# Expert layers of a Sinkhorn mixture: activations and operand differences held in the PSUM banks in the first pass

## The chip, the cores and the metric

The kernel runs on one core of one Trainium2 chip, in one launch. Times are device microseconds of that core; the times of a kernel are a median over runs, and one execution of it was profiled.

## The reference

```python
def _moe_ref(x, w_gate, w1, w2):                 # x: 3072 x 512, 8 experts, F = 1024
    logits = x @ w_gate
    logits = logits - logits.max()
    P = np.exp(logits)
    for _ in range(8):
        P /= P.sum(1, keepdims=True) + 1e-09
        P /= P.sum(0, keepdims=True) + 1e-09
        P *= N / E
    for e in range(E):
        h = np.maximum(x @ w1[e], 0.0)
        out += P[:, e:e + 1] * (h @ w2[e])

def reference(**kwargs):
    attn_out = _attn_ref(q, k, v, n_global, n_local)    # banded attention, 4 x 8 x 768 x 64
    x = attn_out.transpose(0, 2, 1, 3).reshape(B * S, H * D)
    return _moe_ref(x, w_gate, w1, w2)
```

Banded attention makes the 3072 rows of 512 numbers that go through eight experts. Each expert's two layers are matrix products with a ReLU between them, and a row's result is weighted by its share P of the expert.

## The kernel before

The hidden dimension of all experts is cut into 31 groups of two 128-wide tiles (`groups`, `NG` = 31) and the rows into three passes (`NB` = 3). The first four groups (`PLAIN` = 4) of the first pass run in a stage of their own, between the attention and the loop that the change is about. That loop (`for n, (what, p, x, y) in enumerate(todo)`) runs pass 0 over groups 4 to 29 in 13 pairs, here called chunks, and over group 30, called plain; then passes 1 and 2 over all groups.

Both expert layers are computed by a seven-product (Strassen and Winograd) scheme. Every operand of a product is held as a high part, rounded to a 32-bit matmul format, and a rest (full value minus high part), and every product takes three matmuls per tile. Layer 1 of a group (`layer1_scaled`, "a first" below) makes the products m3, m2, m1, m6, m5, m4 and m7, six matmuls each, in four PSUM banks c, d, a, b (c, d and a are used twice). VectorE puts them together in two running sums t3 and t1; `scaled` applies the ReLU and the share and writes the four blocks h22, h12, h21, h11 to SBUF; the differences d7 = h12 - h22, d5 = h22 - h21, d6 = h12 - d5 and d4 = d6 - h11 are formed from them. Each of the seven results becomes an operand p1 to p7 of layer 2: `high` is a ScalarE cast, `rest` subtracts that cast from the result. In pass 0 (`prepares`) all differences and rests run on VectorE; in passes 1 and 2 on GpSimd.

Layer 2 (`second_layer`) runs over a chunk's two groups in two parts: p3, p7, p5, p1 in the chunk itself, and p6, p4, p2 behind the even first of the next chunk ("behind" below). So the order on TensorE is, chunk by chunk: even first (42 matmuls), behind of the chunk before (36), odd first (42), second (48). Four sums (p3, p7, p6, p4; `SEEDED`) are copied into their bank by ScalarE ahead of the matmuls and copied out behind them; the other three are added by VectorE (L1500).

In pass 0 the weights' operands are made on the way (`make_blocks`): a DMA on SyncE's queue brings a raw tile (`raw`, two buffers), GpSimd forms the scheme's sums (`ext`, and `raw` in place; L1380, L1398), ScalarE casts the high parts (L1410), GpSimd subtracts for the low parts (L1411), and the block `wb` (a ring of five) is also written to DRAM (L1043), from where passes 1 and 2 load it. Blocks are asked for two items of `todo` ahead.

A scheduler orders each engine's instructions, but for those recorded through `Ordered`, which keep the program's order. Line 68 is `Ordered`'s, so that all its operations stand at L68.

Of the kernel before, what the change touches and what calls it, by code (L numbers as in the profile page):

```python
# [17 lines left out]
P = 128  # L18
# [5 lines left out]
UT = 3  # L24
# [572 lines left out]
class Moe:  # L597
# [173 lines left out]
    def layer1_scaled(self, x, blocks, share, full, ops, tmp, ps, tag, waits, used, begins, soon, plain, prepares):  # L771
# [7 lines left out]
        if prepares:  # L779
            gp = Ordered(self.tc, nc.vector).tensor_tensor  # L780
# [97 lines left out]
        rest("p2", h11, other)  # L878

# [116 lines left out]
def pipeline(tc, attention, ident, moe, acc, scratch):  # L996
# [12 lines left out]
    with ExitStack() as top:  # L1009
# [243 lines left out]
        def second(g, hs, halves=(0, 1)):  # L1253
            e, b = groups[g][0], passes[0]
            first_scaled = e != 0 and groups[g - 1][0] == 0
            for i in halves:
                for t in range(WT):
# [3 lines left out]
                    if t == 2:  # L1261
                        beat()
# [8 lines left out]
                    if g == PLAIN - 1:  # L1271
                        u, n = divmod(tt, UT)
                        nc.sync.dma_start(out=y_spill[u][:, n], in_=a)
# [20 lines left out]
        for g in range(PLAIN):  # L1294
# [22 lines left out]
            if g == PLAIN - 1:  # L1317
                spill_rows()
            if g == 1:
                second(*prev, (0,))  # L1320
                second(g, hs, (0,))
                moe.act = nc.scalar
            elif g == 2:
                second(*prev, (1,))
            elif prev is not None:
                second(*prev)
            prev = (g, hs)
        second(*prev)
        load_share(0, groups[PLAIN][0])
# [35 lines left out]

        def make_blocks(g, layer, part):

            e, f = groups[g]
            gp = nc.gpsimd.tensor_tensor
            base, (lo, hi) = 7 * layer, ((0, SPLIT), (SPLIT, 7))[part]  # L1370
            if layer == 0:
                if part == 0:
                    raw = wstage.tile([P, KT, FG * P], F32, name="raw")
                    nc.sync.dma_start(out=raw, in_=moe.w1[e, :, f * P:(f + FG) * P].rearrange("(c p) f -> p c f", p=P))
# [12 lines left out]
            elif g == NG - 1:  # L1387
                raw = wstage.tile([P, FG, DM], F32, name="raw")
                nc.sync.dma_start(out=raw, in_=moe.w2[e, f * P:(f + FG) * P, :].rearrange("(f p) d -> p f d", p=P))
                parts = ((slice(0, 4), raw.rearrange("p f (d c) -> p (f d) c", d=2), None),)  # L1390
            elif part == 0:
                raw = wstage.tile([P, FG, DM], F32, name="raw")
                nc.sync.dma_start(out=raw, in_=moe.w2[e, f * P:(f + FG) * P, :].rearrange("(f p) d -> p f d", p=P))
# [8 lines left out]
            else:  # L1402
                raw = wstage.tile([P, FG, DM], F32, name="raw")
                nc.sync.dma_start(out=raw[:, 0], in_=moe.w2[e, f * P:(f + 1) * P, :])
                nc.sync.dma_start(out=raw[:, 1, 0:FULL], in_=s2_spill[g])
# [14 lines left out]
        def first_layer(p, g):  # L1420
# [15 lines left out]

            return moe.layer1_scaled(ops, lambda i: blocks_of[g, 0, i], share, free if begins else full, ops_of[g], tmp, mps, "h",
# [212 lines left out]
```

## Time and profile before

| | us |
|---|---|
| median of 3 runs (lowest, highest) | 2208.03 (2207.44, 2209.78) |
| the profiled execution: its own time | 2207.4 |
| its span | 2205.5 |
| mean granted TensorE clock, share of full speed | 0.976 |

| engine | busy us | share of the span |
|---|---|---|
| TensorE matmul (PE) | 2091.2 | 95% |
| GpSimd (POOL) | 1660.7 | 75% |
| VectorE (DVE) | 1535.0 | 70% |
| ScalarE (ACT) | 863.2 | 39% |

The page's 40 slices show TensorE at eight or nine tenths up to about 1000 us and at nine or more behind that; VectorE's digits fall there from eight to five or six. The loop begins at 363 us (first matmul of group 4), and pass 0 ends at 1008 us. The rows below are from that stretch, and from pass 1 for comparison. In the timeline rows, the columns are start, duration, engine, line, operation, tiles and count, and in brackets the idle time ahead of it with what ended it.

### The profile page before, as it was taken

To read this page: it belongs to the slowest core of one execution; us is meant where nothing else is said; L and a number is where in the kernel's file an instruction comes from. 1 tells how busy PE (TensorE), PEld (TensorE's weight loads), DVE (VectorE), ACT (ScalarE), POOL (GpSimd) and SP (SyncE) were. 2 spreads that over 40 slices of the span, in tenths; PEclk is the share of its full clock that TensorE was granted. 3 is DMA by queue.
4 is the path that set the end of the run, shared out by engine and by line. 5 is a ranking of instruction groups with operands and counts; after the bars stand their busy time and mean duration, and the time that the engine had idled before them with its cause. 6 is when DMAs were issued, how large, how long until landed. Compare 5 with 4: busy or idle time off the path is not lost.

```text
span 2205.5 us, 30538 instructions
## 1 busy us (share of the span) xinstructions
PE 2091.2 (95%) x10365; PEld 1726.9 (78%) x10365; DVE 1535.0 (70%) x2534; ACT 863.2 (39%) x1832; POOL 1660.7 (75%) x1441
## 2 busy tenths in 40 slices
PE   8999997889888888879999999999999999999998
PEld 6888885667776677768888888888888888888887
DVE  8777775888888888876556655665656655655566
ACT  7777533555554555522322222222142222222221
POOL 6787974887888887884777767676867676767776
PEclk9999998999999899989999999999999999999999
DMA  6777475667666666679656566565785665656564
GB/s 156 211 216 206 156 272 189 222 217 251 225 234 230 229 222 239 219 275 341 210 193 207 179 209 209 201 209 191 281 300 188 210 210 186 212 193 212 182 209 158
DMA packets 229157, 477.49 MB, mean 216 GB/s; under 512 B 107072, under 2 KB 152576, under 8 KB 205696
## 3 DMA queue, kind: packets, MB, share of 16 engines
q1 hardware_dynamic: 228704, 474.40, 63.6%
q8 instruction: 84, 1.38, 0.3%
q0 software_dynamic: 288, 1.05, 0.1%
q14 instruction: 81, 0.66, 0.1%
HBM read 328.75 MB, written 146.64 MB: 216 GB/s over the span
## 4 chain that ended last, share of the span: by engine, by line
PE 68%; POOL 13%; issue 6%; DMA 5%; DVE 4%; ACT 4%; SPq 0%; POOLq 0%; DVEq 0%; ACTq 0%
PE c_acc L124 28%; PE bank_c L124 8%; PE bank_a L124 8%; PE bank_d L124 8%; POOL wb L1411 6%; PE bank_b L124 4%; DMA raw<-in_moe_w_dram 4%; POOL ext L1398 2%; PE o_t L124 2%; POOL ext L1380 2%; ACT p_sb L369 2%; POOL raw L1380 1%; PE o_ps L124 1%; PE s_ps L124 1%; PE y_ps L124 1%
## 5 line engine op out<-in xcount | busy, mean ns | idle before, releaser
L124 PE MATMUL c_acc<-p,wb 128*128 128x512 f32 x2838 | 703.4, 401 | 69.7 <-DVE p L68 65.2
L124 PEld LDWEIGHTS c_acc<-p,wb 128*128 128x128 f32 x2838 | 549.6, 194 | 195.7 <-issue 61.5
L796 ACT CAST p<-full 128x512 fp32r<-128x512 f32 x384 | 226.3, 621 | 697.1 <-DVE full L793 423.9
L1500 DVE TENSOR_TENSOR early<-early,c_acc 128x512 f32<-128x512 f32 x363 | 246.0, 685 | 182.5 <-PE c_acc L124 182.4
L68 POOL TENSOR_TENSOR p<-full,p 128x512 fp32r<-128x512 f32 x270 | 347.8, 1304 | 5.0 <-ACT p L796 4.7
L124 PE MATMUL bank_c<-x,wb 128*128 128x512 f32 x1068 | 275.2, 393 | 16.9 <-ACT wb L1410 10.0
L68 POOL TENSOR_TENSOR early<-full,full 128x512 f32<-128x512 f32 x56 | 72.9, 1301 | 287.6 <-DVE full L793 287.6
L124 PE MATMUL bank_a<-m,wb 128*128 128x512 f32 x1068 | 273.1, 391 | 5.3 <-DVE early L806 4.7
L124 PE MATMUL bank_d<-x,wb 128*128 128x512 f32 x1068 | 273.0, 391 | 0.0
L124 PEld LDWEIGHTS bank_c<-x,wb 128*128 128x128 f32 x1068 | 202.5, 190 | 60.5 <-ACT wb L1410 10.4
L124 PEld LDWEIGHTS bank_a<-m,wb 128*128 128x128 f32 x1068 | 201.3, 189 | 48.5 <-DVE early L806 5.6
L124 PEld LDWEIGHTS bank_d<-x,wb 128*128 128x128 f32 x1068 | 202.0, 189 | 42.4
L68 POOL TENSOR_TENSOR full<-full,full 128x512 f32<-128x512 f32 x172 | 222.8, 1296 | 0.0
L124 PE MATMUL c_acc<-x,wb 128*128 128x512 f32 x774 | 197.6, 390 | 1.6 <-ACT early L1498 1.6
L1411 POOL TENSOR_TENSOR wb<-raw,wb 128x512 fp32r<-128x512 f32 (+2 forms) x133 | 169.1, 1287 | 38.3 <-ACT wb L1410 32.4
L804 DVE TENSOR_TENSOR early<-early,bank_d 128x512 f32<-128x512 f32 x89 | 61.0, 686 | 195.2 <-PE bank_d L124 185.4
L124 PEld LDWEIGHTS c_acc<-x,wb 128*128 128x128 f32 x774 | 144.5, 188 | 33.8 <-ACT early L1498 4.4
L68 DVE TENSOR_TENSOR p<-full,p 128x512 fp32r<-128x512 f32 x117 | 147.8, 1280 | 13.6 <-ACT p L796 12.3
L1411 POOL TENSOR_TENSOR wb<-ext,wb 128x512 fp32r<-128x512 f32 (+1 forms) x80 | 123.8, 1548 | 28.1 <-ACT wb L1410 28.1
L124 PE MATMUL bank_b<-m,wb 128*128 128x512 f32 x534 | 135.6, 389 | 0.5 <-DVE extra L793 0.5
L796 ACT CAST x<-full 128x512 fp32r<-128x512 f32 x123 | 76.5, 624 | 107.7 <-POOL full L68 91.0
L124 PEld LDWEIGHTS bank_b<-m,wb 128*128 128x128 f32 x534 | 100.2, 188 | 21.7 <-DVE extra L793 0.9
(354 smaller groups left out, 3519.3 us busy)
## 6 DMA issues: line engine op xcount, KB each, us to landing
wb<-ws SPq DMA_DIRECT2D x124, 1024.0 KB, 6.7
wb<-ws SPq DMA_DIRECT2D x122, 768.0 KB, 4.2
ws<-wb SPq DMA_DIRECT2D x54, 1024.0 KB, 4.2
ws<-wb SPq DMA_DIRECT2D x53, 768.0 KB, 4.3
raw<-in_moe_w_dram SPq DMA_DIRECT2D x54, 512.0 KB, 5.5
x<-p_rows SPq DMA_DIRECT2D x21, 512.0 KB, 5.3
x<-op_m SPq DMA_DIRECT2D x16, 512.0 KB, 9.7
ws<-w SPq DMA_DIRECT2D x4, 1792.0 KB, 8.4
```

The lines of the kernel that those rows point to most:

```text
L68: return lambda *args, **kw: self.tc.keep_in_program_order(op(*args, **kw))
L124: return self.tc.keep_in_program_order(self.engine.matmul(*args, **kw))
L369: scalar.activation(out=views[u], in_=views[u], func=AF.Exp, bias=mx[:, u:u + 1], scale=-1.0, accum_out=sm[:, i, j:j + 1])
L796: engine.copy(out=ops[k][:, 0], in_=src)
L804: tt(out=t3, in0=t3, in1=d, op=ALU.subtract)
L1380: gp(out=to, in0=x, in1=y, op=op)
L1398: gp(out=to, in0=x, in1=y, op=op)
L1411: gp(out=low, in0=src, in1=high, op=ALU.subtract)
L1500: nc.vector.tensor_tensor(out=sums[k][q], in0=sums[k][q], in1=bank, op=ALU.add)
```

## The change

In pass 0, firsts of groups 4 to 29 use a new function, `layer1_held`. It writes the scaled blocks h12 and h21 back into their banks c and d, forms d7 in bank b, d6 in bank c and d4 in bank a, and `high` and `rest` read them there; only h22, h11 and d5 are in SBUF. A bank is then held until the last reader is through. All of its VectorE operations keep the program's order, and the rest of p2 goes to GpSimd. `prepares` is gone from `layer1_scaled`, so that the plain group's four rests and its join go to GpSimd. `raw_weights` asks for a raw tile when the one before it is taken. In the stage ahead of the loop, `beat()` is called at two more places, `spill_rows()` a group earlier, and the eight DMAs that spill the accumulators stand with `load_share(0)` behind the first two items' loads.

```diff
-    def layer1_scaled(self, x, blocks, share, full, ops, tmp, ps, tag, waits, used, begins, soon, plain, prepares):
+    def layer1_scaled(self, x, blocks, share, full, ops, tmp, ps, tag, waits, used, begins, soon, plain):
...
-        if prepares:
-            gp = Ordered(self.tc, nc.vector).tensor_tensor
...
+    def layer1_held(self, x, blocks, share, full, ops, tmp, ps, tag, used):
...
+        vector = Ordered(self.tc, nc.vector)
+        tt, copy = vector.tensor_tensor, nc.scalar.copy
...
+        h22, h11, d5 = full
...
+        def scaled(out, src, i):
+            vector.scalar_tensor_tensor(out=out, in0=src, scalar=0.0, in1=share[:, i], op0=ALU.max, op1=ALU.mult)
+
+        def high(k, src):
+            copy(out=ops[k][:, 0], in_=src)
+
+        def rest(k, src, engine=tt):
+            engine(out=ops[k][:, 1], in0=src, in1=ops[k][:, 0], op=ALU.subtract)
+
+        product("m3", "c", True, False)
+        copy(out=t3, in_=c)
+        product("m2", "d", True, False)
+        tt(out=t3, in0=t3, in1=d, op=ALU.subtract)
+        product("m1", "a", True, False)
+        tt(out=t4, in0=a, in1=t3, op=ALU.add)
+        product("m6", "b", True, True)
+        tt(out=b, in0=b, in1=t4, op=ALU.add)
+        scaled(h22, b, 1)
+        product("m5", "c", False, True)
+        tt(out=t3, in0=t3, in1=c, op=ALU.subtract)
+        scaled(c, c, 1)
+        high("p3", c)
+        tt(out=b, in0=c, in1=h22, op=ALU.subtract)
+        high("p7", b)
+        rest("p3", c)
+        product("m4", "d", False, True)
+        tt(out=t3, in0=d, in1=t3, op=ALU.add)
+        scaled(d, d, 0)
+        tt(out=d5, in0=h22, in1=d, op=ALU.subtract)
+        high("p5", d5)
+        high("p1", d)
+        rest("p7", b)
+        product("m7", "a", False, True)
+        used("share")
+        tt(out=a, in0=a, in1=t3, op=ALU.add)
+        scaled(h11, a, 0)
+        rest("p1", d)
+        rest("p5", d5)
+        yield
+        tt(out=c, in0=c, in1=d5, op=ALU.subtract)
+        high("p6", c)
+        tt(out=a, in0=c, in1=h11, op=ALU.subtract)
+        high("p4", a)
+        high("p2", h11)
+        rest("p6", c)
+        rest("p4", a)
+        rest("p2", h11, nc.gpsimd.tensor_tensor)
...
-                    if t == 2:
+                    if t % 2 == 0:
                         beat()
...
+        def raw_weights(g, layer, part):
...
         def make_blocks(g, layer, part):
...
+            if layer or part == 0:
+                while raws and raws[0][0] != (g, layer, part):
+                    raws.pop(0)
+                if not raws:
+                    raws.append(((g, layer, part), raw_weights(g, layer, part)))
+                raw = raws.pop(0)[1]
+                after = wanted[wanted.index((g, layer, part)) + 1:][:1]
+                raws.extend((a, raw_weights(*a)) for a in after if a[0:2] != (g, 1))
...
+            if p == 0 and g < NG - 1:
+                return moe.layer1_held(ops, lambda i: blocks_of[g, 0, i], share, (full[0], full[3], full[4]), ops_of[g], tmp, mps, "h", used)
+
...
         for item in todo[0:2]:
             loads(*item)
+        load_share(0, groups[PLAIN][0])
+        for j in range(BT):
+            u, t = divmod(passes[0] * BT + j, UT)
+            nc.sync.dma_start(out=y_spill[u][:, t], in_=acc[:, j])
```

The order of the instructions on TensorE is the same before and after. On SyncE's queue the raw tiles' DMAs stand in the same places among the others, and what moves in the loop are five loads of the shares, by three rows each. On the other engines the order changes as in these three places.

VectorE, end of an even first and the behind part's last product p2 (its sums are `extra`), before, and then after. `bank_a` to `bank_d` are PSUM tiles; `p` and `x` take the rests, L804 is t3 of the odd first.

```order
L68 TENSOR_TENSOR p<-full_5682,p 128x512
L1500 TENSOR_TENSOR extra_5686<-extra_5686,c_acc 128x512
L1500 TENSOR_TENSOR extra_5687<-extra_5687,c_acc 128x512
L68 TENSOR_TENSOR full_5680<-full_5681,full_5684 128x512
L68 TENSOR_TENSOR p<-full_5684,p 128x512
L68 TENSOR_TENSOR full_5681<-full_5680,full_5683 128x512
L68 TENSOR_TENSOR x_169<-full_5680,x_169 128x512
L804 TENSOR_TENSOR early<-early,bank_d 128x512
L806 TENSOR_TENSOR early<-bank_a,early 128x512
L68 TENSOR_TENSOR x_171<-full_5681,x_171 128x512
L68 TENSOR_TENSOR x_172<-full_5683,x_172 128x512
L808 TENSOR_TENSOR bank_b<-bank_b,early 128x512
```

```order
L68 TENSOR_TENSOR p<-bank_d,p 128x512
L68 TENSOR_TENSOR p<-full_5675,p 128x512
L1568 TENSOR_TENSOR extra_5677<-extra_5677,c_acc 128x512
L1568 TENSOR_TENSOR extra_5678<-extra_5678,c_acc 128x512
L68 TENSOR_TENSOR bank_c<-bank_c,full_5675 128x512
L68 TENSOR_TENSOR bank_a<-bank_c,full_5674 128x512
L68 TENSOR_TENSOR x_169<-bank_c,x_169 128x512
L68 TENSOR_TENSOR x_171<-bank_a,x_171 128x512
L68 TENSOR_TENSOR early<-early,bank_d 128x512
L68 TENSOR_TENSOR early<-bank_a,early 128x512
```

The additions from `c_acc` now stand ahead of both differences d6 and d4 and of the last two rests, which read and write the banks, and the rest of p2 is gone.

ScalarE at the same place, before and then after: `x` takes the high parts of p2, p6 and p4, `c_acc` rows copy the sums into their banks for the second part, and L802 (after: L900) copies m3 of the odd first.

```order
L1482 COPY c_acc<-early 128x512 x2
L796 CAST x_172<-full_5683 128x512
L1482 COPY c_acc<-early 128x512 x2
L802 COPY early<-bank_c 128x512
L796 CAST x_169<-full_5680 128x512
L1410 CAST wb<-ext 128x3x256
L796 CAST x_171<-full_5681 128x512
L1410 CAST wb<-raw 128x256
```

```order
L894 CAST x_172<-full_5674 128x512
L1475 CAST wb<-ext 128x3x256
L1550 COPY c_acc<-early 128x512 x2
L900 COPY early<-bank_c 128x512
L894 CAST x_169<-bank_c 128x512
L1475 CAST wb<-raw 128x256
L894 CAST x_171<-bank_a 128x512
```

The cast of three sums of a weights' block (`wb` from `ext`), which stood behind the copies and the first of the high parts after them (`x_169`), now stands ahead of them.

GpSimd, making the blocks for layer 2 and layer 1 of a coming chunk, after (before has the same rows without the one at L897).

```order
L1466 TENSOR_TENSOR ext<-raw 128x256 x2
L1466 TENSOR_TENSOR raw<-ext,raw 128x256
L1466 TENSOR_TENSOR ext<-raw 128x256
L897 TENSOR_TENSOR x_172<-full_5674,x_172 128x512
L1476 TENSOR_TENSOR wb<-ext,wb 128x3x256
L1466 TENSOR_TENSOR ext<-raw 128x256 x2
```

The rest of p2 stands between the last sum of a block and that block's low part.

## Rows read from the trace of the kernel before

**Rows 1.** Busy time in three stretches: span, then busy (count) by engine, clock, DMA, GB/s.

```profile
363.18:545.25 182.07, 159.86 (x637) 126.66 (x637) 153.09 (x182) 96.56 (x184) 153.70 (x138) 0.92 0.64 228
545.25:920.90 375.65, 325.70 (x1345) 262.71 (x1344) 329.63 (x385) 200.66 (x384) 317.86 (x274) 0.92 0.65 230
1027.93:1066.15 38.22, 38.22 (x169) 31.45 (x168) 17.97 (x27) 17.68 (x33) 28.02 (x23) 1.00 0.72 260
```

**Rows 2.** Timeline of TensorE, one chunk of pass 0: odd first, then second.

```profile
657.07 1.52 PE L124 MATMUL bank_c<-x,wb 128*128 128x512 f32 x6
...
666.59 1.52 PE L124 MATMUL c_acc<-p,wb 128*128 128x512 f32 x6
674.23 12.11 PE L124 MATMUL c_acc<-p,wb 128*128 128x512 f32 x42 [6.12 <-DVE p L68]
```

**Rows 3.** Waits from 545.25 to 920.90: engine, line and releaser, total us, times, longest.

```profile
PE c_acc L124 <- DVE p L68: 48.1, 8, 6.1
POOL wb L1411 <- ACT wb L1410: 34.7, 24, 3.1
```

**Rows 4.** VectorE by form, 545.25 to 920.90: busy us, mean ns, idle time ahead.

```profile
L68 DVE TENSOR_TENSOR p<-full,p 128x512 fp32r<-128x512 f32 x73 | 95.7, 1328 | 9.6 <-ACT p L796 9.6
L68 DVE TENSOR_TENSOR full<-full,full 128x512 f32<-128x512 f32 x48 | 46.8, 976 | 0.0
L68 DVE TENSOR_TENSOR x<-full,x 128x512 fp32r<-128x512 f32 x24 | 34.3, 1455 | 10.0 <-ACT x L796 10.0
L68 DVE TENSOR_TENSOR p<-early,p 128x512 fp32r<-128x512 f32 x16 | 20.1, 1257 | 0.0
L68 DVE TENSOR_TENSOR early<-full,full 128x512 f32<-128x512 f32 x16 | 13.4, 838 | 0.0
L808 DVE TENSOR_TENSOR bank_b<-bank_b,early 128x512 f32<-128x512 f32 x16 | 11.1, 692 | 5.3 <-PE bank_b L124 5.3
```

**Rows 5.** Timeline of GpSimd and of VectorE at the same time, in that chunk.

```profile
656.63 2.53 POOL L1411 TENSOR_TENSOR wb<-raw,wb 128x512 fp32r<-128x512 f32 x2
656.58 1.37 DVE L1500 TENSOR_TENSOR extra<-extra,c_acc 128x512 f32<-128x512 f32 x2 [0.51 <-PE c_acc L124]
```

**Rows 6.** GpSimd by form, 545.25 to 920.90, as in Rows 4.

```profile
L1411 POOL TENSOR_TENSOR wb<-raw,wb 128x512 fp32r<-128x512 f32 x49 | 71.5, 1460 | 22.6 <-ACT wb L1410 19.4 <-PE bank_b L124 3.2
L1380 POOL TENSOR_TENSOR ext<-raw 128x256 f32<-128x256 f32 x48 | 48.5, 1037 | 17.4 <-DMA raw<-in_moe_w_dram 16.8
```

**Rows 7.** Timeline of GpSimd at the start of pass 0, VectorE idle.

```profile
365.56 0.74 POOL L1411 TENSOR_TENSOR wb<-ext,wb 128x256 fp32r<-128x256 f32 x1
366.25 1.28 POOL L1411 TENSOR_TENSOR wb<-raw,wb 128x512 fp32r<-128x512 f32 x1
```

**Rows 8.** Timeline of SyncE and GpSimd: a raw tile asked for, and its first reader.

```profile
641.61 0.41 SPq L1374 DMA_DIRECT2D raw<-in_moe_w_dram  x1
647.97 2.69 POOL L1380 TENSOR_TENSOR ext<-raw 128x256 f32<-128x256 f32 x3 [2.11 <-DMA raw<-in_moe_w_dram]
```

**Rows 9.** Timeline of TensorE: start of group 5, and short waits in the first chunks.

```profile
377.73 1.52 PE L124 MATMUL bank_c<-x,wb 128*128 128x512 f32 x6
388.66 1.66 PE L124 MATMUL bank_a<-m,wb 128*128 128x512 f32 x6 [1.72 <-DVE early L806]
439.42 7.78 PE L124 MATMUL c_acc<-p,wb 128*128 128x512 f32 x33 [1.19 <-DVE p L68]
```

**Rows 10.** Timeline of ScalarE around the end of the behind part at 657.07.

```profile
656.51 1.13 ACT L1482 COPY c_acc<-early 128x512 f32<-128x512 f32 x2
...
663.45 0.84 ACT L1410 CAST wb<-ext 128x768 fp32r<-128x768 f32 x1 [3.22 <-POOL ext L1398]
```

**Rows 11.** Timeline of TensorE: last chunk of pass 0, and the plain group.

```profile
920.90 1.52 PE L124 MATMUL bank_c<-x,wb 128*128 128x512 f32 x6
...
976.40 0.39 PE L124 MATMUL bank_c<-x,wb 128*128 128x512 f32 x1
981.97 2.50 PE L124 MATMUL bank_c<-x,wb 128*128 128x512 f32 x5 [5.18 <-POOL wb L1411]
```

More of the change, by code (lines that the diff above doesn't have):

```diff
@@ L878, in layer1_scaled @@
         rest("p2", h11, other)
+    def layer1_held(self, x, blocks, share, full, ops, tmp, ps, tag, used):
+        nc = self.nc
+        vector = Ordered(self.tc, nc.vector)
+        tt, copy = vector.tensor_tensor, nc.scalar.copy
+        bank = {n: ps.tile([P, WIDE], F32, name=f"bank_{n}", tag=tag) for n in "cdab"}
+        product = self.block_products(bank, x, blocks)
+        a, b, c, d = (bank[n] for n in "abcd")
+        t3, t4 = tmp
+        h22, h11, d5 = full
[43 more added lines that the diff above has]
+        rest("p2", h11, nc.gpsimd.tensor_tensor)
     def layer1_strassen(self, x, w, hs, tmp, ps, tag, sums_first, beat):
@@ L1364, in load_blocks @@
                 blocks_of[g, layer, n] = t[:, n - lo]
-        def make_blocks(g, layer, part):
-            e, f = groups[g]
+        def raw_weights(g, layer, part):
+            e, f = groups[g]
+            raw = wstage.tile([P, KT, FG * P] if layer == 0 else [P, FG, DM], F32, name="raw")
+            w2 = moe.w2[e, f * P:(f + FG) * P, :].rearrange("(f p) d -> p f d", p=P)
+            if layer == 0:
+                nc.sync.dma_start(out=raw, in_=moe.w1[e, :, f * P:(f + FG) * P].rearrange("(c p) f -> p c f", p=P))
+            elif part == 0:
+                nc.sync.dma_start(out=raw, in_=w2)
+            else:
+                nc.sync.dma_start(out=raw[:, 0], in_=w2[:, 0])
+                nc.sync.dma_start(out=raw[:, 1, 0:FULL], in_=s2_spill[g])
+            return raw
+        def make_blocks(g, layer, part):
+            if layer or part == 0:
[6 more added lines that the diff above has]
+                raws.extend((a, raw_weights(*a)) for a in after if a[0:2] != (g, 1))
             gp = nc.gpsimd.tensor_tensor
@@ L1372, in make_blocks @@
                 if part == 0:
-                    raw = wstage.tile([P, KT, FG * P], F32, name="raw")
-                    nc.sync.dma_start(out=raw, in_=moe.w1[e, :, f * P:(f + FG) * P].rearrange("(c p) f -> p c f", p=P))
                     staged_of[g] = raw, wstage.tile([P, 3, KH, P], F32, name="ext", bufs=1)
```

33 lines of the change are left out of this document (12 added, 21 removed).

## The prediction

> **What bounds the kernel now.** I read the page's slices first: TensorE is full from about 1000 us on and short of it ahead of that. So I looked for what it waits for in pass 0, by the busy time of stretches, then the waits, then one chunk's timeline. Eight chunks, from the first matmul of one even first to that of the ninth, last 375.65 us, 46.96 each [rows 1]. The same matmuls without a wait last 38.22 in pass 1, at clock 1.00 [rows 1]. The excess of 8.7 has one place. In each of the eight chunks the second, after its first product of the even group, stands still for about 6.1 us for a rest that VectorE writes: 48.1 us in all, 8 times [rows 3]. The 42 matmuls behind it take 12.11 us where 38.22 x 42/168 = 9.6 is the full-speed time: 2.5 more, at a lower granted clock (0.92 over the stretch, against 1.00) [rows 1, 2]. 6.1 + 2.5 = 8.6. Passes 1 and 2 are full; nothing of this change reaches them.
>
> Who is late is VectorE: busy 329.63/8 = 41.2 us a chunk, more than TensorE's 38.2 [rows 1]. GpSimd has 39.7 [rows 1]. They make each other slow. VectorE's eleven operations a first with both inputs in SBUF come to 95.7 + 46.8 + 34.3 + 20.1 + 13.4 = 210.3 over 16 firsts, 13.1 us a first, mean 1.19 each; one with an input in a bank takes 0.69 [rows 4]. GpSimd's subtraction of 512 columns takes 1.46 on average and its sum of 256 columns 1.04 [rows 6], but 1.28 and 0.74 with VectorE idle [rows 7], and two of the former take 2.53 while VectorE adds from a bank at 1.37 for two [rows 5]: that pairing costs neither.
>
> **The change part by part.** *Operands in the banks.* Of the eleven, one goes to GpSimd (rest of p2), nine get a bank operand, and one (rest of p5) keeps two SBUF inputs. At 0.69 and, for the last, 1.2: 9 x 0.69 + 1.2 = 7.4 instead of 13.1 a first, so VectorE falls by 11.4 a chunk to about 30, eight below TensorE. The 6.1 us wait goes, with the slow clock behind it.
>
> *GpSimd.* Without that contention its 39.7 shrinks in about the ratio 1.28/1.46 to 0.74/1.04, to 28 to 35, and it gains two rests, 2 x 1.28 = 2.6: 31 to 37, I take 34. It also waits: 34.7/8 = 4.3 a chunk for ScalarE's casts [rows 3], and 16.8/8 = 2.1 for a raw tile [rows 6]. 34 + 4.3 + 2.1 = 40.4: from now on GpSimd is as near to the bound as TensorE.
>
> *Raw tiles.* Their DMAs keep their places on SyncE's queue, behind the same writes of blocks, with two buffers as before. A tile asked for at 641.61 has its first reader at 647.97 [rows 8]; I expect that 6.4 and the wait of about 2.1 to stay, and count nothing. Nor do I count the start of the pass: what stands ahead of the first raw tile is the same.
>
> *A new wait at the end of the even first.* Call T the end of the behind part. The additions of p2 wait for T, and d6, the rests of p6 and p4 now stand behind them on VectorE, while the odd first's third product needs the bank that the rest of p6 frees. The two additions end at T + 1.3 [rows 5], d6 at T + 2.0, its cast (ScalarE, 0.6, in the same bank, so d4 must wait for it) at T + 2.7, d4 at T + 3.3 and the rest of p6 at T + 4.0. TensorE wants the bank after two products, at T + 2.7. So it stands for about 1.3. What that does to the clock I take from the nearest rows: a wait of 1.72 left six matmuls at 1.66 instead of 1.52, and one of 1.19 left 33 at 7.78, where 33 x 0.2275 = 7.5 [rows 9]: 0.1 to 0.3, I take 0.2. The bounds are 0, if ScalarE and VectorE come sooner, and the 2.5 of the old wait.
>
> *ScalarE's queue.* At that place a cast of weights now stands ahead of the copies of sums and the cast for p6. It waits for GpSimd's sums. Before, they were ready at 663.45, T + 6.4 [rows 10], without harm; now each microsecond of lateness behind about T goes on to TensorE. Its raw tile came at 647.97, T - 9.1 [rows 8], asked for once the low part before it was done. Half a chunk of GpSimd's work leads up to that point, 39.7/2, and shortens by about a fifth, so I put the tile 4 us sooner, at T - 13. From there to the last sum GpSimd has 11 instructions of 256 columns and 3 of 512, 11 x 0.74 + 3 x 1.28 = 12.0 [rows 7]: T - 1, just in time. Bounds 0 and 6.4; I take 0.8, nearer to the first.
>
> A chunk is then 38.2 + 1.3 + 0.2 + 0.8 = 40.5.
>
> *The sum,* against the profiled 2207.4: eight chunks save 8 x (46.96 - 40.5) = 51.7. The four before them last 182.07 [rows 1]. The first has no behind part but starts slowly: its even first takes until 377.73, 14.6 from 363.18 [rows 1, 9], and keeps that; with 9.5 for the odd first, 11.0 for the second and about 7.5 of new waits (no behind part covers its banks: about 3 for the rest of p7, 2 for that of p6, and 2.5 at the slow clock) it takes 42.5. 182.07 - (42.5 + 3 x 40.5) = 18.1. The last chunk, with all of its second layer, lasts 55.5 from 920.90 to 976.40 [rows 11]; 40.5 + 8.2 = 48.7 saves 6.8. In the plain group, the 5.18 wait for its weights [rows 11] shrinks, since GpSimd comes sooner, but four rests (4 x 1.28 = 5.1) and a join of 2.5 are now on GpSimd ahead of the last products: I count nothing, from -3 to +3. 51.7 + 18.1 + 6.8 = 76.6, so 2130.8; the median stands 0.6 above the profiled run: **2131**.
>
> **A rule against it.** In the changed program, d7 waits for ScalarE's cast of p3 and d4 for that of p6, each out of the bank that it reads, though the data don't ask for it; at about 0.6 a cast that is 2.4 a chunk, of which the sum has one 0.6 on the path. The trace of before has no such wait, as both read SBUF there. The Trainium skill, page "PSUM — Partial Sum Buffer", section "PSUM bank collisions raise a hardware error", says why: two engines may not touch one bank and quadrant at once, reads included, so that dependencies stand between ScalarE and VectorE too. By it, with all four casts on the path, the sum would be 12 x 1.8 = 22 longer, 2153.
>
> **The rivals.** *A, the forecast:* chunks of 39.6 to 41.5, 2118 to 2144. *B, GpSimd and ScalarE become the bound:* the casts of 0.6 stand in series with VectorE at both firsts (1.8 more), and GpSimd's sums come late by another 1.2. For it: GpSimd's sum of work and waits is already at the chunk's length, and the raw tile's 6.4 stays. Against: its waits for ScalarE are partly VectorE's lateness, and shrink with it. At 43.5 a chunk and 44.5 for the first it saves 8 x 3.46 + 7.1 + 3.8 = 38.6: 2169. *C, nothing waits any more:* ScalarE and GpSimd run ahead and the bank comes nearly in time; 39.0 a chunk and 41.5 for the first save 63.7 + 23.6 + 8.3 = 95.6: 2112. Full cover, 38.2, would give about 2103. *D, slower:* GpSimd keeps its old phase, T + 6.4. Then ScalarE's cast ends at T + 7.2, its two copies at T + 8.4 (1.13 [rows 10]), that of m3 at T + 9.0, the cast for p6 at T + 9.6, d4 and the rest of p6 at T + 10.8: TensorE stands for 8.1, and its clock falls by the old 2.5. A chunk is 38.2 + 8.1 + 2.5 = 48.8, 1.8 more than now, and twelve of them give 2229. It decides from a wait of 6.3 on (38.2 + 6.3 + 2.5 = 47), that is from sums later than T + 4.6. Against it: GpSimd's work falls by a fifth, and a standing TensorE lets it catch up. *E, no net relief:* GpSimd's period stays at 47 because every wait it loses turns up at ScalarE; 2208.
>
> **How the numbers follow.** A 0.46, B 0.25, C 0.18, D 0.05, E 0.04, and 0.02 for a small gain between B and E. The predicted time is A's. The range leaves out D, E, the slow end of B and the best of C: 2106 to 2172. About 0.2% is what a measurement of this kernel can tell from no change. Faster by more: A, B, C and the small gain, 0.91; the same: 0.04; slower: 0.05.
>
> **What would show it.** In the profile after: VectorE's operations at L68 in pass 0 at 0.69 with only the rest of p5 above it; GpSimd's 512 columns at 1.28 to 1.30; VectorE's busy time about 30 a chunk; no 6 us wait in the second, and instead 1 to 2 us ahead of the odd first's third product, released by VectorE; raw tiles still some 6 us from issue to first reader. Passes 1 and 2 should last what they do now. I am wrong if the sums of L1466 end well behind T, with TensorE waiting 3 us or more in the odd first, or if the second still waits for a rest because ScalarE's casts were held by GpSimd.

## The result, and the profile after

The changed kernel takes 2121.51 us in the median of four runs (2117.67 to 2124.53), against 2208.8 of the kernel before, run beside it: a ratio of 0.9604, with a 95% interval of 0.9587 to 0.9621. The forecast was 2131, with a range of 2106 to 2172. The time lies 9.5 us below the forecast and inside A's span of 2118 to 2144. The profiled execution below is the fastest of the four, 13.1 us under the 2130.8 of the sum, and the table by stage goes by it.

The profiled execution took 2117.67 us, with a span of 2115.8 and a mean granted clock of 0.993, so it is to be set against the profiled 2207.4 of before. First the same stretches as in [rows 1]: the first four chunks, the next eight, and passes 1 and 2. The columns are the stretch, its length, the busy time of PE, PEld, DVE, ACT and POOL with counts, the granted clock, the DMA share and GB/s.

```profile
363.11:523.88 160.77, 151.53 (x636) 121.98 (x637) 113.21 (x175) 96.62 (x184) 137.98 (x147) 0.96 0.75 264
523.88:840.66 316.78, 307.28 (x1345) 251.56 (x1344) 237.94 (x369) 202.35 (x384) 273.43 (x289) 1.00 0.77 273
919.85:2115.80 1195.95, 1190.90 (x5291) 986.24 (x5289) 717.08 (x1050) 307.16 (x518) 861.09 (x681) 1.00 0.62 210
```

Against [rows 1] the eight chunks fell from 375.65 to 316.78 us, 39.60 each. TensorE now works 307.28 of the 316.78 at clock 1.00, where it worked 325.70 at 0.92. VectorE's 329.63 became 237.94 and GpSimd's 317.86 became 273.43. Passes 1 and 2 are what they were (1197.49 before). The whole difference of 89.7 us by stage, from the first matmuls of the chunks:

| stage | before | after | saved | forecast |
|---|---|---|---|---|
| first four chunks | 182.07 | 160.77 | 21.3 | 18.1 |
| eight chunks | 375.65 | 316.78 | 58.9 | 51.7 |
| last chunk, 920.90 to 976.40; after, 840.66 to 892.09 | 55.50 | 51.43 | 4.1 | 6.8 |
| plain group, up to the first matmul of pass 1 | 31.61 | 27.76 | 3.9 | 0 |
| passes 1 and 2 | 1197.49 | 1195.95 | 1.5 | 0 |

One chunk's timeline on TensorE answers [rows 2]: the end of the behind part is T = 581.06, then come the odd first and the second.

```profile
581.06 1.52 PE L124 MATMUL bank_c<-x,wb 128*128 128x512 f32 x6
582.42 1.52 PE L124 MATMUL bank_d<-x,wb 128*128 128x512 f32 x6
585.07 1.65 PE L124 MATMUL bank_a<-m,wb 128*128 128x512 f32 x6 [1.13 <-DVE x L68]
...
592.00 11.04 PE L124 MATMUL c_acc<-p,wb 128*128 128x512 f32 x48
602.88 1.52 PE L124 MATMUL bank_c<-x,wb 128*128 128x512 f32 x6
```

The wait of 6.12 us in the second is gone: all its 48 matmuls run in one piece. The one that is left is the forecast's new one, ahead of the odd first's third product, released by the rest of p6 on VectorE. It is 1.13 us long, and the six matmuls behind it take 1.65 instead of 1.52.

The forms of VectorE in the eight chunks, to be read against [rows 4] (busy us, mean ns, and the idle time ahead with what ended it):

```profile
L68 DVE TENSOR_TENSOR p<-bank_c,p 128x512 fp32r<-128x512 f32 x24 | 16.3, 678 | 0.0
L68 DVE TENSOR_TENSOR p<-full,p 128x512 fp32r<-128x512 f32 x16 | 13.9, 871 | 0.0
L68 DVE TENSOR_TENSOR bank_b<-bank_c,full 128x512 f32<-128x512 f32 x16 | 11.2, 699 | 12.4 <-ACT p L894 12.4
L68 DVE TENSOR_TENSOR bank_a<-bank_c,full 128x512 f32<-128x512 f32 x16 | 11.1, 696 | 9.5 <-ACT x L894 9.5
```

With one operand in a bank, a rest or a difference takes 0.68 to 0.70 us, where its predecessors with both in SBUF took 0.84 to 1.46. The rest of p5 alone (the second row) keeps two SBUF inputs, at 0.87. GpSimd's forms, against [rows 6]:

```profile
L1476 POOL TENSOR_TENSOR wb<-raw,wb 128x512 fp32r<-128x512 f32 x48 | 65.6, 1367 | 12.5 <-ACT wb L1475 12.5
L1452 POOL TENSOR_TENSOR ext<-raw 128x256 f32<-128x256 f32 x48 | 34.2, 743 | 8.4 <-DMA raw<-in_moe_w_dram 7.8
```

The 256 columns are at 0.74, the value of [rows 7] with VectorE idle, down from 1.04. The 512 columns came from 1.46 to 1.37 on average. In GpSimd's timeline 41 of these 48 take about 1.30, and seven, one in each of seven chunks, take 1.74 to 1.78: each of the seven runs beside the rest of p5 on VectorE, the one operation that is left with two inputs in SBUF (for one, GpSimd from 557.77 for 1.78 us, VectorE from 557.72). So both engines gained from the one move, GpSimd without any change in what it does there.

### The profile page after: what moved, and what is told of

It is laid out like the page before. It is cut to its first block, busy times and chain, and to the rows that moved or that the text cites. A ratio compares the mean times of both kernels' runs of the same rounds, so it can differ in the third digit from the quotient of the medians.

```text
span 2115.8 us, 30545 instructions
## 1 busy us (share of the span) xinstructions
PE 2063.2 (98%) x10365; PEld 1710.2 (81%) x10365; DVE 1393.7 (66%) x2504; ACT 863.9 (41%) x1832; POOL 1598.5 (76%) x1471
## 4 chain that ended last, share of the span: by engine, by line
PE 72%; POOL 4%; DMA 2%; ACT 1%; issue 1%; DVE 1%; SPq 0%; POOLq 0%; DVEq 0%; ACTq 0%
PE c_acc L124 34%; PE bank_a L124 10%; PE bank_c L124 10%; PE bank_d L124 10%; PE bank_b L124 5%; PE o_t L124 2%; POOL wb L1476 2%; DMA raw<-in_moe_w_dram 2%; POOL ext L1466 1%; POOL early L1578 0%; DMA s<-raw 0%; POOL raw L1452 0%; ACT x L894 0%; POOL ext L1452 0%; DVE bank_a L68 0%
## 5 line engine op out<-in xcount | busy, mean ns | idle before, releaser
L124 PE MATMUL c_acc<-p,wb 128*128 128x512 f32 x2838 | 673.3, 390 | 3.6 <-POOL p L897 2.5
L124 PEld LDWEIGHTS c_acc<-p,wb 128*128 128x128 f32 x2838 | 532.1, 188 | 116.8 <-DVE p L68 3.6
L794 ACT CAST p<-full 128x512 fp32r<-128x512 f32 x271 | 159.8, 621 | 578.9 <-DVE full L791 343.5
L1476 POOL TENSOR_TENSOR wb<-raw,wb 128x512 fp32r<-128x512 f32 (+2 forms) x133 | 148.8, 1135 | 20.3 <-ACT wb L1475 19.5
L802 DVE TENSOR_TENSOR early<-early,bank_d 128x512 f32<-128x512 f32 x63 | 43.3, 687 | 152.0 <-PE bank_d L124 152.0
L1476 POOL TENSOR_TENSOR wb<-ext,wb 128x512 fp32r<-128x512 f32 (+1 forms) x80 | 103.8, 1298 | 14.2 <-ACT wb L1475 14.2
L68 POOL TENSOR_TENSOR x<-full,x 128x512 fp32r<-128x512 f32 x87 | 110.2, 1296 | 0.0
L1568 DVE TENSOR_TENSOR extra<-extra,c_acc 128x512 f32<-128x512 f32 x109 | 74.2, 686 | 50.1 <-PE c_acc L124 50.1
```

The lines of the kernel that those rows point to most:

```text
L68: return lambda *args, **kw: self.tc.keep_in_program_order(op(*args, **kw))
L124: return self.tc.keep_in_program_order(self.engine.matmul(*args, **kw))
L794: engine.copy(out=ops[k][:, 0], in_=src)
L802: tt(out=t3, in0=t3, in1=d, op=ALU.subtract)
L1476: gp(out=low, in0=src, in1=high, op=ALU.subtract)
L1568: nc.vector.tensor_tensor(out=sums[k][q], in0=sums[k][q], in1=bank, op=ALU.add)
```

## The experiments

The order of TensorE's instructions is the same in all of these kernels. "Chunk" is the mean of the eight chunks after the first four; ratios are to the kernel before, with their 95% intervals. The theory under test (O in the expectations) is that the place of the operands is the cause. The rivals are that the fixed order, the rest moved to GpSimd, or the earlier raw tiles carry the gain.

**Order without the place.** `sbuf_ordered` is the changed kernel with the blocks and differences in SBUF again, in the same fixed order, and with the rest of p2 still on GpSimd.

```diff
-        h22, h11, d5 = full
+        h22, h12, h21, h11, d5 = full
+        d7, d6, d4 = t4, h22, h12
...
-        scaled(c, c, 1)
-        high("p3", c)
-        tt(out=b, in0=c, in1=h22, op=ALU.subtract)
+        scaled(h12, c, 1)
+        high("p3", h12)
+        tt(out=d7, in0=h12, in1=h22, op=ALU.subtract)
...
```

> The changed kernel with one thing undone: the scaled blocks and the differences go to SBUF buffers again, in the new fixed order and with the rest of p2 still on GpSimd. Theory O (the gain comes from operands in the banks, which end the mutual slowing of VectorE and GpSimd): VectorE's operations with two SBUF inputs are back at about 1.2 us, its busy time at about 38 us a chunk, TensorE waits for a rest in the second again, chunks of 42 to 47 us, 2150 to 2210. Theory R (the gain comes from the fixed order on VectorE and the rest of p2 moved away): chunks stay at 39.5, time within 6 us of the changed kernel's 2121.5.

It took 2221.88 us (2219.39 to 2224.48), a ratio of 1.0062 [1.0046, 1.0079]: the whole gain is gone, and 0.6% more. That is past the slow end of what the theory had expected. Its VectorE and GpSimd forms in the eight chunks are slow again:

```profile
L68 DVE TENSOR_TENSOR p<-full,p 128x512 fp32r<-128x512 f32 x64 | 71.0, 1129 | 19.6 <-ACT p L895 19.6
L68 DVE TENSOR_TENSOR full<-full,full 128x512 f32<-128x512 f32 x48 | 53.1, 1106 | 1.1
```

```profile
L1477 POOL TENSOR_TENSOR wb<-raw,wb 128x512 fp32r<-128x512 f32 x48 | 70.2, 1464 | 20.5 <-ACT wb L1476 20.5
L1453 POOL TENSOR_TENSOR ext<-raw 128x256 f32<-128x256 f32 x48 | 46.0, 985 | 12.9 <-DMA raw<-in_moe_w_dram 12.2
```

GpSimd's two means are back at those of [rows 6] within some 5%, with VectorE at the same operations in the same order. That two inputs in SBUF are not slow by themselves shows in the kernel before, where such a difference runs at 0.68 us while GpSimd stands idle (VectorE's timeline, then GpSimd's, which does nothing from 961.97 to 965.81):

```profile
962.50 0.68 DVE L68 TENSOR_TENSOR full<-full,full 128x512 f32<-128x512 f32 x1
```

```profile
965.81 1.67 POOL L1510 TENSOR_TENSOR early<-early 128x512 f32<-128x512 f32 x1 [3.84 <-DVE early L1500]
```

So the slowness belongs to the pair of engines with operands in SBUF. In `sbuf_ordered` VectorE is busy 39.3 us a chunk, and the chunk is 47.89. The wait, though, is another than before. TensorE's longest waits in the eight chunks (engine, line and releaser, total us, times, longest, as in [rows 3] and in all such rows below):

```profile
PE c_acc L124 <- ACT wb L1476: 22.8, 6, 4.8
PE c_acc L124 <- POOL wb L1477: 11.0, 11, 1.6
```

So with all of the change but the place it is the weights that come late, and VectorE's order is no gain by itself. ScalarE's order is not the changed kernel's here: its cast of the three sums stands behind the copies again. `d6_first` below has it there too, at 40.88 a chunk with the operands in the banks, so that the 47.89 is not made by that cast's place alone.

The Trainium skill, page "SBUF — State Buffer", section "Who interferes with whom", states that a VectorE instruction with two SBUF inputs contends with a GpSimd instruction that reads SBUF, and one with at most one SBUF input, outside the 2-port performance modes, does not. The runs agree: GpSimd's 256 columns take 0.99 us on average here and 0.74 in the changed kernel, and its 512 columns there exceed 1.4 only beside the rest of p5. The section gives no measured time for this pairing.

**The place without the rest.** `held_only` is the kernel before, with `layer1_held` alone added; the raw tiles, the spills, the beats and the plain group are as before.

```diff
+            if p == 0 and g < NG - 1:
+                return moe.layer1_held(ops, lambda i: blocks_of[g, 0, i], share, (full[0], full[3], full[4]), ops_of[g], tmp, mps, "h", used)
```

> The kernel before with only the new first-layer function of pass 0 put in: no raw tiles asked for ahead, the spills, loads and beats where they were, and the plain group's rests and join on VectorE as before. Theory O: the chunks are 39.5 as in the changed kernel, and the time within 5 us of it, on the lower side if the plain group's waits for GpSimd (about 4 us at the end of pass 0) go: 2113 to 2124. Theory Q (asking for the raw tiles ahead carries part of the gain): a raw tile is waited for longer than 1 us a chunk, chunks of 41 or more, over 2135.

2119.14 us (2115.92 to 2121.45), 0.9594 [0.9578, 0.961], with a chunk of 39.93. All of the gain is in `layer1_held`; the other parts of the change add nothing that can be measured here. The prediction had counted nothing for them.

**The rest of p2.** `p2_on_vector` puts the one rest that the change had moved to GpSimd on VectorE again, in `layer1_held`'s fixed order.

```diff
-        rest("p2", h11, nc.gpsimd.tensor_tensor)
+        rest("p2", h11)
```

> The changed kernel with the rest of p2 on VectorE, in the fixed order, instead of GpSimd. Theory O: VectorE has about 9 us of idle time in a chunk of 39.5 and takes two more operations of 0.7 to 1.3 at no cost, GpSimd is 2.6 us lighter: 2115 to 2128, chunks 39.5 or a little less or more by where the operation stands. Theory P (moving p2 away carried the gain): chunks longer by 2 us or more, over 2145.

2121.18 us (2120.64 to 2123.21), 0.9611 [0.9595, 0.9627]: no difference in the total. The chunk is 40.31, 0.7 longer, because a second small wait joins the first (waits from 520 to 840 us, nearly the eight chunks):

```profile
PE bank_a L124 <- DVE x L68: 9.5, 8, 1.3
PE c_acc L124 <- DVE p L68: 3.1, 7, 0.6
```

The last chunk gives some of it back, 49.25 us against 51.43: TensorE's wait for that rest at the end of pass 0 (2.53 us in the changed kernel, shown below) is gone, and one of 0.68 for a cast of ScalarE stands earlier in that chunk.

**The wait that is left.** The bank wait could go if the differences came ahead of the behind part's additions. `early_d6` moves the `yield` behind everything but the rest of p2. The edit does more than I meant: the behind part, which uses the same operands, then multiplies the new group's p6 and p4 (so its time is to be read with that).

```diff
         rest("p5", d5)
-        yield
         tt(out=c, in0=c, in1=d5, op=ALU.subtract)
...
         rest("p4", a)
+        yield
         rest("p2", h11, nc.gpsimd.tensor_tensor)
```

> The changed kernel with d6, d4, their casts and the rests of p6 and p4 moved ahead of the point at which the behind part is written down, so that VectorE does them ahead of the additions of p2. Theory O with the bank wait as forecast (the 1.13 us at the third product of every odd first comes from the additions standing ahead of d6): that wait goes, chunks 38.2 to 38.5, 11 chunks x 1.2 = 13 us less, 2105 to 2111. Theory G (GpSimd, or ScalarE behind it, paces the chunk at 39.5): the wait turns up elsewhere, time within 3 us of 2121.5.

2220.69 us (2219.77 to 2221.05), 1.0058 [1.0041, 1.0075]; the expectation missed. TensorE waits in every chunk for operands that have only just been begun (its timeline):

```profile
616.16 2.93 PE L124 MATMUL c_acc<-x,wb 128*128 128x512 f32 x6 [8.29 <-ACT x L894]
```

It says nothing about the bank wait, but something on the clock: right behind the 8.29 us these six matmuls take 2.93 instead of 1.52, at a granted clock of 0.50 from 616.16 to 619.00. That is the 1.2 GHz level.

`d6_first` moves only the two differences, with no cast and no rest, and leaves the operands as they are.

```diff
-        yield
         tt(out=c, in0=c, in1=d5, op=ALU.subtract)
-        high("p6", c)
         tt(out=a, in0=c, in1=h11, op=ALU.subtract)
+        yield
+        high("p6", c)
         high("p4", a)
```

> The changed kernel with only the two differences d6 and d4 (which write banks, not operands) moved ahead of the behind part, the casts and rests of p6 and p4 left behind it. In this program ScalarE's casts of p6 and p4 also come ahead of its copies of sums. Theory O: the rest of p6 ends at T + 2.0, ahead of T + 2.7, the 1.13 us wait of every odd first goes, chunks 38.2 to 38.5, 2106 to 2112. Theory G (GpSimd's work and waits pace the chunk at 39.5): the wait goes and another takes its place, 2118 to 2124.

2132.72 us (2131.66 to 2135.16), 0.9663 [0.9647, 0.9679]: the bank wait is gone, and the kernel is 11 us slower for it, with a chunk of 40.88. TensorE now waits in the second, for the weights' blocks:

```profile
PE c_acc L124 <- POOL wb L1476: 10.7, 8, 1.4
PE c_acc L124 <- ACT wb L1475: 3.9, 4, 1.8
PE c_acc L124 <- ACT early L1566: 1.5, 2, 0.8
```

So another bound takes the place of the bank wait. It can't have stood hidden behind it in this length: the changed kernel's chunk is 39.60, and this one is 40.88. The edit brought it, or the order that the scheduler then chose. In this program the scheduler has put ScalarE's cast of three sums behind the copies again, and the block's second cast behind those for p3 and p7. Either the blocks are late because GpSimd has too much to do, or because ScalarE's casts of them now stand too late in its order. The second cast itself is not what is late: in seven of the eight chunks ScalarE stands idle ahead of it, 0.2 to 1.7 us, until GpSimd's sums are there (at 674.12, 0.95 us).

**How much room GpSimd has.** `pool_plus` does the rest of p2 three times, some 5.2 us of GpSimd more a chunk.

```diff
         rest("p2", h11, nc.gpsimd.tensor_tensor)
+        rest("p2", h11, nc.gpsimd.tensor_tensor)
+        rest("p2", h11, nc.gpsimd.tensor_tensor)
```

> The changed kernel with the rest of p2 computed three times by GpSimd instead of once: 4 more operations of 1.3 us a chunk, 5.2 us. Theory B (GpSimd with its work and waits is as near to the bound as TensorE, as the prediction's 40.4 says): chunks 3 to 5 us longer, 2155 to 2180. Theory S (GpSimd has slack, its waits shrink when it has more to do): under 2 us a chunk, below 2145.

2150.81 us (2147.86 to 2155.97), 0.9746 [0.9725, 0.9767]; the chunk is 42.22, 2.6 longer for 5.2 of work, between the two expectations. So about half of it found room, and the rest came out as waits for the weights in the second, with a clock of 0.98 in place of 1.00:

```profile
PE bank_a L124 <- DVE x L68: 10.3, 8, 2.0
PE c_acc L124 <- POOL wb L1478: 9.1, 8, 1.4
PE c_acc L124 <- ACT wb L1477: 2.3, 6, 1.1
```

At this place in its order GpSimd has about 2.6 us of room in a chunk of 39.6.

`d6_first_p2` is `d6_first` with the rest of p2 on VectorE, so that GpSimd has 2.6 us less to do.

> d6_first with the rest of p2 on VectorE too: GpSimd has 2.6 us a chunk less to do, while ScalarE's order stays that of d6_first: the cast of the second weights' block's sums stands behind the odd first's casts of p3 and p7. In d6_first TensorE waits in the second for that block (0.3 to 1.8 us for ScalarE's cast, then 1.4 for GpSimd's low part). Theory K (the place of that cast in ScalarE's queue makes the wait): it stays, chunks about 40 to 41, 2122 to 2134. Theory L (GpSimd's load makes it): it goes, chunks 38.3 to 38.8, 2106 to 2114.

2124.55 us (2120.12 to 2127.15), 0.9623 [0.9604, 0.9643]; the chunk is 40.53. Taking 2.6 us of work from GpSimd (its busy time fell by 1.5 a chunk, 259.15 for 271.48 in eight) gave 0.35 a chunk, and the wait for the weights is still there:

```profile
PE c_acc L124 <- POOL wb L1476: 7.8, 6, 1.4
PE c_acc L124 <- ACT wb L1475: 3.1, 3, 1.7
```

The time and the chunk are those that theory K had named, and not L's: the amount of GpSimd's work is not all of it. But K's mechanism does not hold as it was put. In six of the eight chunks ScalarE stands idle ahead of the cast in question, 0.3 to 4.8 us, for GpSimd's sums. GpSimd in its turn waits for ScalarE's casts of weights, 49.3 us in the eight chunks, where the changed kernel has 20.1, or 33.0 with its waits for the casts of p2. The longest of these waits stands at the head of a chunk, for a cast behind ScalarE's copies (GpSimd's waits, then its timeline):

```profile
POOL wb L1476 <- ACT wb L1475: 49.3, 28, 4.3
```

```profile
604.80 1.99 POOL L1476 TENSOR_TENSOR wb<-raw,wb 128x512 fp32r<-128x512 f32 x2 [4.29 <-ACT wb L1475]
```

At the like place in the changed kernel GpSimd does the rest of p2 first and then waits 1.77 for that cast, until 605.26: the 2.6 us taken from GpSimd there became a longer wait.

`c_first_p2` moves one difference only (d6 ahead of the `yield`, d4 behind it), with the rest of p2 on VectorE. It was meant to bring ScalarE's cast of the weights ahead of that for p3.

> Only d6 (not d4) ahead of the behind part, and the rest of p2 on VectorE. In this program ScalarE's cast of the second weights' block's sums stands ahead of the cast of p3, as in the changed kernel, and the cast of p6 comes ahead of the copies of sums. Theory K: neither the bank wait (the rest of p6 ends at about T + 2.5, ahead of T + 2.7) nor a wait for that block; chunks 38.3 to 38.9, 2106 to 2114. Theory L agrees here, so that this run and d6_first_p2 together tell them apart. Rival: another wait of about 1 us takes the place in either, 2118 to 2124.

2124.99 us (2121.92 to 2126.65), 0.9624 [0.9608, 0.964], with a chunk of 40.11. The cast stood ahead of that for p3 in only three of the eight chunks. In these three TensorE waits for no weights, and in the other five for 1.0 to 2.1 us; but in all eight ScalarE had stood idle ahead of that cast for GpSimd's sums, so that an early cast and a wait that stays away may both come of early sums. So this is no test of ScalarE's order, and it is inconclusive. It does show the exchange once more: the bank wait has almost gone (0.6 us once), and `PE c_acc <- POOL wb` has come, with 6.2 in all.

**The end of pass 0.** `plain_dve` puts the plain group's rests and join on VectorE again, and the rest of p2 of groups 28 and 29 too.

```diff
+        if prepares:
+            gp = Ordered(self.tc, nc.vector).tensor_tensor
...
-        rest("p2", h11, nc.gpsimd.tensor_tensor)
+        rest("p2", h11, tt if last else nc.gpsimd.tensor_tensor)
```

> The changed kernel with the end of pass 0 relieved of GpSimd: the plain group's four rests and its join on VectorE again, and the rest of p2 of groups 28 and 29 on VectorE. Theory O: the 2.53 us wait at the last product of the last chunk and the 1.8 us in the plain group's last products go with the slow clock behind them, 4 to 6 us: 2115 to 2118. Rival: the weights' low parts on GpSimd, which are then what comes last, keep it there: within 2 us of 2121.5.

2120.18 us (2119.47 to 2122.51), 0.9604 [0.9588, 0.962]: no gain. The wait only moved, to GpSimd's last sums (TensorE's timeline):

```profile
905.86 0.47 PE L124 MATMUL o_t<-ident,early 128*128 128x128 f32 x1 [4.13 <-POOL early L1580]
```

`best`, this and `d6_first` together, behaves like `d6_first`.

> d6_first and plain_dve together. If both mechanisms hold and add: 12 to 19 us below the changed kernel, 2102 to 2110. If GpSimd paces the chunk: 2114 to 2120.

2132.86 us (2129.87 to 2134.62), 0.9657 [0.9641, 0.9673].

**Two bounds.** The last pair takes the weights' low parts out of GpSimd's work: it fills them with zeros instead of subtracting, so the results lack that part. `low0_changed` is the changed kernel with that edit alone, and `low0_d6_first_p2` is the same on `d6_first_p2`.

```diff
-                gp(out=low, in0=src, in1=high, op=ALU.subtract)
+                nc.gpsimd.memset(low.bitcast(F32), 0.0)
```

> The changed kernel with the low parts of the weights' blocks made in pass 0 left out of the computation: GpSimd fills them with zeros instead of subtracting, so that it has less to do and doesn't wait for ScalarE's casts there. The bank wait of the odd first is untouched. Theory M (in the changed kernel the bank wait of 1.13 us sets the 39.5 us chunk, and the making of weights is hidden just behind it): chunks stay at 39.5, 2112 to 2122, the rest of the gain at most from the start and the end of pass 0. Theory G (the weights pace it): chunks below 39, 2105 to 2112.

> d6_first_p2 with the same low parts left out of the computation (zeros). There the bank wait is gone and TensorE waits for a weights' block in the second. Theory M: with the making of weights relieved too nothing is left to wait for, chunks 38.1 to 38.4, about 1.2 us x 12 = 14 less than low0_changed, 2098 to 2108. Theory G': another wait of about 1 us takes its place (VectorE's or ScalarE's casts in the second): chunks about 39.5, within 3 us of low0_changed.

`low0_changed` took 2108.89 us (2106.83 to 2110.95), 0.9556 [0.954, 0.9572]. Its eight chunks are no faster, 39.74 each, although GpSimd's busy time fell from 273.43 to 178.14 (columns as in [rows 1]):

```profile
519.39:837.31 317.92, 307.30 (x1346) 251.75 (x1344) 236.62 (x369) 202.78 (x386) 178.14 (x289) 1.00 0.78 271
```

TensorE's one wait in them is the bank's, 10.6 us in all in eight pieces. So in the changed kernel the bank wait sets the chunk and the weights do not. The total is lower than theory M had it, in the span that theory G had named, but not for G's reason: what this kernel gained lies at the ends of pass 0, 2.9 us in the first four chunks and 6.9 in the last chunk and the plain group (837.31 to 909.61, where the changed kernel has 840.66 to 919.85).

`low0_d6_first_p2` took 2091.19 us (2089.71 to 2092.87), 0.9476 [0.946, 0.9491], and its eight chunks are full:

```profile
516.72:821.36 304.64, 304.64 (x1346) 252.34 (x1344) 251.15 (x385) 202.32 (x384) 163.33 (x273) 1.00 0.80 283
```

38.08 us a chunk, with TensorE busy all of it; the time is below the expected 2098 to 2108. Set side by side: without the bank wait a chunk is 40.53, without the weights' work 39.74, without both 38.08. Neither removal alone shortens the chunk: without the weights' work the bank wait stays, and with the differences ahead the weights come late. What stays open is how near the weights are to the bound in the changed kernel's own order, and which part of the path that makes them is the bound when the differences stand ahead. GpSimd and ScalarE wait for each other there, and no run moves a cast alone. Filling with zeros shortens GpSimd's chain and also takes away its waits for those casts, so it does not tell the two apart. A longer ring of weight blocks was not tried.

None of these kernels that computes all of the result is faster than the changed one by more than their runs overlap.

## Why the prediction was right, and where it was off

**The cause** was right. VectorE and GpSimd slowed each other with both inputs in SBUF, and the place of the operands is what took it away. `sbuf_ordered` and `held_only` show it from both sides.

**Durations.** VectorE's forecast of about 30 us a chunk is 237.94/8 = 29.7. GpSimd's 34 is 273.43/8 = 34.2, within its bounds of 31 to 37. The rest of p5, put at 1.2, took 0.87.

**The new wait.** Its forecast of 1.3 us measured 1.13, for reasons that do not quite hold. VectorE and ScalarE at T = 581.06:

```profile
580.58 1.37 DVE L1568 TENSOR_TENSOR extra<-extra,c_acc 128x512 f32<-128x512 f32 x2 [1.48 <-PE c_acc L124]
581.87 0.69 DVE L68 TENSOR_TENSOR bank_c<-bank_c,full 128x512 f32<-128x512 f32 x1
583.73 0.70 DVE L68 TENSOR_TENSOR bank_a<-bank_c,full 128x512 f32<-128x512 f32 x1 [1.17 <-ACT x L894]
584.34 0.68 DVE L68 TENSOR_TENSOR x<-bank_c,x 128x512 fp32r<-128x512 f32 x1
```

```profile
580.72 0.83 ACT L1475 CAST wb<-ext 128x768 fp32r<-128x768 f32 x1
581.46 1.11 ACT L1550 COPY c_acc<-early 128x512 f32<-128x512 f32 x2
582.62 0.59 ACT L900 COPY early<-bank_c 128x512 f32<-128x512 f32 x1
583.11 0.59 ACT L894 CAST x<-bank_c 128x512 fp32r<-128x512 f32 x1
```

The additions did not wait for T. They began at T - 0.5, so d6 was done at T + 1.5, not at T + 2.0. The row that the prediction cites for T + 1.3 shows this already: 656.58 + 1.37 is T + 0.9, as T was 657.07. But ScalarE's copy of m3 stands ahead of the cast for p6 (rival D counts that copy, the forecast does not), and m3's six matmuls end only at 581.06 + 1.52 = 582.58. So the copy began at 582.62, and the cast for p6 ran from T + 2.05 to T + 2.6. The rest of p6 ended at T + 4.0, as forecast: two errors of about 0.5 cancel. The clock behind it cost 1.65 - 1.52 = 0.13, for a forecast of 0.2.

**The step that was mis-sized** is ScalarE's queue, at 0.8 a chunk. The cast of the sums stands at 580.72, ahead of the copies as the instruction order says. Its sums were ready at T - 0.5, for an estimate of T - 1, and that was soon enough: the copy of m3, with which the next piece of the path begins on ScalarE, could not have begun before 582.58 anyway. It was so with nothing to spare, as the two copies ahead of it end at 582.57. In seven of the eight chunks that term measured 0. In one the sums came later, the cast began at 738.97 for T = 739.06, and the bank wait was 1.25 instead of 1.13: the mechanism is there, at 0.1 us in one chunk. So a chunk without the term is 38.2 + 1.3 + 0.2 = 39.7, and it measured 39.60. Over eight chunks the term's 0.8 is 6.4 us of the 7.2 that the sum lacked there (58.9 against 51.7).

**GpSimd "as near to the bound as TensorE"**, by 34 + 4.3 + 2.1 = 40.4, was too strict for the changed kernel. The waits shrank, as one of the sentences on rival B had it. From the waits of the eight chunks and the forms above, 20.1/8 = 2.5 us for the casts and 7.8/8 = 1.0 for a raw tile; 34.2 + 2.5 + 1.0 = 37.7 (below, GpSimd's waits, as in [rows 3]). A new wait that neither the prediction nor this sum counts is that for ScalarE's casts of p2, which came with its rest: (10.9 + 2.0)/8 = 1.6, and with it the sum is 39.3 of a chunk of 39.60. But an engine's work and waits come near the chunk in any kernel, since it does the one or the other all the time, so that such a sum does not tell a bound. `low0_changed` does, in which the chunk stays with 11.9 us less of GpSimd's work in it, and `pool_plus`, which finds room for only 2.6 us: GpSimd was near the bound and not at it. Rival B was wrong on the time, and right in part on where to look.

```profile
POOL wb L1476 <- ACT wb L1475: 20.1, 16, 1.8
POOL p L897 <- ACT p L894: 10.9, 9, 1.7
```

**Raw tiles.** Expected to stay some 6.4 us from issue to first reader: the one asked for at 562.09 is read from 568.38 on, after 6.3 us, with GpSimd's wait at 1.14. SyncE's timeline, and then GpSimd's:

```profile
562.09 0.45 SPq L1425 DMA_DIRECT2D raw<-in_moe_w_dram  x1
```

```profile
568.38 2.14 POOL L1452 TENSOR_TENSOR ext<-raw 128x256 f32<-128x256 f32 x3 [1.14 <-DMA raw<-in_moe_w_dram]
```

**The two ends of pass 0** were a little wrong in opposite directions (TensorE's timeline below: first chunk, last chunk, plain group). The first chunk took 40.7 us (363.11 to 403.80) against the forecast of 42.5. Its wait for the rest of p7 came, and at half the clock behind it (2.93 us for six matmuls), but the one of about 2 for p6 did not. The last chunk saved 4.1, not 6.8: the last p2 waits for its rest, which is now GpSimd's. The prediction had taken that rest only as work, and had not asked who waits for it in the one chunk that has no next one behind it.

```profile
380.00 2.93 PE L124 MATMUL bank_c<-x,wb 128*128 128x512 f32 x6 [3.20 <-DVE p L68]
...
890.24 2.05 PE L124 MATMUL c_acc<-p,wb 128*128 128x512 f32 x6 [2.53 <-POOL p L897]
...
905.49 0.96 PE L124 MATMUL o_t<-wb,p 128*128 128x512 f32 x3 [1.54 <-POOL p L68]
```

The plain group saved 3.9 where the prediction counted nothing, from -3 to +3. Its 5.18 us wait for weights [rows 11] is gone, and a shorter one for a rest on GpSimd (1.54) is there in its place. `held_only`, which has the old plain group, shows no loss in the total. The 1.5 us of passes 1 and 2 have no explanation here; they are of the size by which runs differ.

**The rule on banks.** The Trainium skill, page "PSUM — Partial Sum Buffer", section "PSUM bank collisions raise a hardware error", says that an access of ScalarE and one of VectorE to the same bank and quadrant must not overlap. The waits that follow from it are there: in the forms above VectorE stands 12.4 us ahead of d7, in 16 firsts, and 9.5 ahead of d4, for ScalarE's casts out of the bank. Ahead of d7 that is 0.8 on average and 0.66 in twelve of the sixteen, near the prediction's 0.6. The 9.5 are eight waits of about 1.2, all in the even firsts, as the cast for p6 begins late there; in the odd firsts there is none, since VectorE's additions fill the time. That is 2.7 a chunk, for the prediction's 2.4. But of the four casts a chunk only the one for p6 lies on the path of TensorE, so that the 2153 of "all four on the path" did not come.

## What to carry to other kernels

When two engines slow each other, look first at where their operands lie, before the order of their work: here a result left in the PSUM bank in which it was made gave 4%, and all the rest of the change without it lost 0.6%. A wait of 6 us that goes may leave a small one that is not worth removing: here the edit that took away the 1.13 us brought a longer one. Do not spend on removing the last microsecond before it is known what is next. An edit on one engine can change the order that a scheduler gives another; look at the casts and copies that share an in-order engine with the work that you move, and at the one chunk at the end that has no other behind it to hide in.

## What the runs showed of the hardware

A VectorE operation of 128x512 that takes 0.68 us with one operand in a bank takes 1.11 to 1.13 on average with both in SBUF while GpSimd works, and GpSimd's 256 columns take 0.99 instead of 0.74 (`sbuf_ordered` against the changed kernel). With both in SBUF and GpSimd idle it takes 0.68 as well (at 962.50 in the kernel before). GpSimd's 512 columns take 1.30, and 1.74 to 1.78 beside one such operation.

The short waits of this kernel cost little clock. A wait of 1.13 us in each chunk of 39.6 leaves the granted clock at 1.00, and the six matmuls behind it 0.13 us longer. Waits of 6.1 us in 47 left 0.92 [rows 1], and behind waits of 3.20 and 8.29 us six matmuls took nearly twice their time (2.93 us for 1.52).
